# An attention and feed-forward kernel: the last token group of the first batch's q loaded apart and handled with the second batch, one PSUM tile for each x product, and the second product begun result by result

## Chip, cores and metric

The kernel runs on one core of a Trainium2 chip. The metric is the device time of one execution in microseconds (us); "span" is the time from the first to the last recorded instruction of a profiled execution, some 1.8 us shorter. A ratio compares runs of the same rounds on the same chip; the traces come from several chips, so times across rounds are compared with care.

## The reference

Shapes are 8 batches, 8 heads, 576 tokens, head size 64. All inputs and the output are float32.

```python
q_s = softmax(q over the head dimension)          # per token
k_s = softmax(k over the sequence)                # per head and channel
kv  = einsum('bhsd,bhse->bhde', k_s, v)
x   = einsum('bhsd,bhde->bhse', q_s, kv)          # -> [4608 tokens, 512]
h   = x @ w_in                                    # 512 -> 2048
g   = h + sin(alpha * h)**2 / (alpha + 1e-9)
out = g @ w_out                                   # 2048 -> 512
```

(The softmaxes subtract the maximum and divide by the sum; I have shortened them here.)

## The kernel before: the parts that matter

Each batch has 9 token groups of 64 tokens (J = 9). The feed-forward part works on tiles of 512 tokens, t = 0 to 8, so tile 0 is the first 8 groups of batch 0, and the ninth group belongs to tile 1. Every engine runs its instructions in the order of the program. The loads of batch 0, and the weights:

```python
for n, t, ii in (("q", q, 0), ("k", k, 0), ("q", q, 1), ("v", v, 0), ("k", k, 1)):
    load0(nc.sync, n, t, ii)                     # 576 KB each, all nine groups
# ... GpSimd: the rest of v, then w_in in blocks, then half of w_out
```

The x products of channels 2 and 3 share one PSUM tile of two banks, and two engines copy out of it:

```python
xp = ps_e.tile([128, 2, MF], F32, name="xp", tag="a")
for e in range(2):
    attn_chunk(0, 2 + e, 0, 8, xp[:, e])
for e in range(2):
    (DVE_CP, ACT_CP)[e](xT[:, 2 + e, 0:MF], xp[:, e])
```

First product of tile 0, for 16 outputs `ni`: matmul, sine on ScalarE, square on one of three engines (the string), combine on VectorE one output behind. Outputs 4, 5, 9, 10, 14, 15 borrow the two buffers of the pool `ps_e`; the others use the four of `ps_h`.

```python
late = {6: lambda: load("q", q, 1, ...), 8: lambda: load_wout(2),
        10: lambda: load_wout(3), 13: lambda: load("k", k, 1, ...)}
for ni in range(nN):
    h_slot(0, ni, "DPPPAPPPAPPPAPPP"[ni], lag, lent)   # D VectorE, P GpSimd, A ScalarE
    flush(lag, 1)
    if ni in late:
        late[ni]()
```

Second product of tile 0, into four accumulators, with the work for batch 1 woven in:

```python
take(os, 10);  # transposes of q's ninth group, ScalarE copies them out
take(os, 10);  # its x products, VectorE copies them out
take(os, 26)
exp_q(1); load("v", v, 1, halves=True); load_batch(2); norm_q(1, [GP, V]); exp_k(1)
# transposes of batch 1's q; cast of v by ScalarE and VectorE; table load for the sine
take(os, 8);  kv_mm(1, 0, ps_e, split=True);  kv_norm(1, 0, 1)
take(os, 2);  kv_mm(1, 1, ps_e, split=True);  kv_norm(1, 1, 2)
# ... x products of batch 1, rest of the second product, then tile 1
```

I call `kv_mm(1, 0)` and `kv_mm(1, 1)` the first and second k-v product.

The softmax here doesn't subtract the row's maximum and nothing guards it: scores larger than these inputs give would overflow.

## Time and profile before

| | before |
|---|---|
| time, median of the first 3 runs | 289.62 us (289.36 to 290.15) |
| span of the profiled run | 287.8 us |
| TensorE busy | 95% |
| TensorE begins tile 1 | 48.66 us |
| v of batch 1 lands, two halves | 42.61, 44.04 us |

The prediction below shows the page and the views that this rests on. One more stretch: TensorE around the step from the first to the second product. In a timeline, the columns are start in us, length in us, engine, line, operation, output<-inputs, shape and count; in brackets stand the idle time before and what ended it.

```profile
25.80 2.75 PE L239 MATMUL hp<-xT,win 128*128 128x512 bf16 x11
28.39 1.96 PE L239 MATMUL hh<-xT,win 128*128 128x512 bf16 x8
30.18 0.38 PE L259 MATMUL hp<-wout,g 128*128 128x512 bf16 x1
31.12 2.10 PE L259 MATMUL hp<-wout,g 128*128 128x512 bf16 x9 [0.56 <-DVE g L255]
```

Outputs 14 and 15 (`hh`) run without a wait from 28.39. After one matmul of the second product, TensorE idles 0.56 us for a combine, which frees the second accumulator.

### The profile page before, as it was taken

Reading aid. Unit: us, or ns where it says so; the run is one execution under the profiler, and the core shown is the slowest. Engines: PE = TensorE matmul, PEld = TensorE weight load, DVE = VectorE, ACT = ScalarE, POOL = GpSimd, SP = SyncE. Lnnn points to the kernel's source line nnn. Section 1 sums busy time; section 2 is a strip of 40 time slices with the busy share of each in tenths; the row PEclk is TensorE's granted clock in tenths of the full one; section 3 lists DMA queues with packets and bytes.
Section 4 is the critical chain, followed back from the end, with each engine's and each line's share of the span. In section 5 each row is a group of like instructions: output and inputs, shape, how many; then the busy total and the mean of one; then the engine's idle time right before and its main releaser. Section 6 shows DMA issues by size and latency. Waiting matters only on the chain.

```text
span 287.8 us, 4228 instructions
## 1 busy us (share of the span) xinstructions
PE 273.8 (95%) x1541; PEld 130.3 (45%) x1569; DVE 188.5 (66%) x281; ACT 225.6 (78%) x317; POOL 82.6 (29%) x78
## 2 busy tenths in 40 slices
PE   2889999999999999999999999999999999999995
PEld 1334454445454445444544454445444444444443
DVE  3948596789958567856776676747674555555412
ACT  4969656999579999899889988998877777777500
POOL 2769620676685662005300440022000000000000
PEclk9999999999999999999999999999999999999999
DMA  7999999855899958119900990115111111111142
GB/s 264 293 194 233 269 391 408 288 203 144 196 171 408 386 174 140 39 37 362 286 20 24 331 343 8 36 40 128 27 39 36 36 36 39 36 36 38 39 110 73
DMA packets 36997, 45.77 MB, mean 159 GB/s; under 512 B 15968, under 2 KB 20336, under 8 KB 36976
## 3 DMA queue, kind: packets, MB, share of 16 engines
q1 hardware_dynamic: 32304, 40.57, 46.0%
q0 software_dynamic: 4480, 4.79, 9.7%
q8 instruction: 12, 0.20, 0.3%
q10 hardware_dynamic: 192, 0.14, 0.2%
q14 instruction: 9, 0.07, 0.1%
HBM read 36.71 MB, written 9.44 MB: 160 GB/s over the span
## 4 chain that ended last, share of the span: by engine, by line
PE 87%; DVE 4%; POOL 3%; ACT 2%; issue 1%; DMA 1%
PE op L259 37%; PE hp L239 36%; PE hp L259 5%; PE kvp L162 3%; POOL s L249 2%; PE xp L211 2%; PE hh L239 2%; DMA st_q<-in_q_dram 1%; PE op L560 1%; PE op L239 1%; ACT s L245 1%; DVE qn L151 1%; DVE qs L149 1%; PE xp L219 1%; DVE g L255 1%
## 5 line engine op out<-in xcount | busy, mean ns | idle before, releaser
L255 DVE SCALAR_TENSOR_TENSOR g<-s,inva_sb,hp 128x512 bf16<-128x512 f32 x130 | 96.2, 746 | 64.6 <-ACT s L247 54.2
L239 PE MATMUL hp<-xT,win 128*128 128x512 bf16 x512 | 129.5, 379 | 1.8 <-DVE kbd L175 1.1
L259 PE MATMUL op<-wout,g 128*128 128x512 bf16 x479 | 121.8, 379 | 1.1 <-issue 0.5
L245 ACT ACTIVATE s<-hp,alpha_sb 128x512 f32<-128x512 f32 x130 | 87.7, 683 | 26.4 <-PE hp L239 24.7
L239 PEld LDWEIGHTS <-win 128*128 128x128 bf16 x576 | 56.0, 98 | 69.5 <-issue 2.1
L259 PEld LDWEIGHTS <-g 128*128 128x128 bf16 x560 | 54.1, 98 | 61.8 <-issue 1.3
L247 ACT ACTIVATE s<-s 128x512 f32<-128x512 f32 x110 | 69.3, 630 | 3.5
L151 POOL TENSOR_TENSOR qn<-qe,qs 128x1152 bf16<-128x1152 bf16 x12 | 25.3, 2128 | 74.5 <-DVE qs L145 63.4
L249 POOL TENSOR_TENSOR s<-s 128x512 f32<-128x512 f32 x31 | 32.4, 1059 | 21.9 <-ACT s L245 21.5
L265 DVE COPY o<-op 128x512 f32<-128x512 f32 (+2 forms) x33 | 22.1, 669 | 9.4 <-PE op L259 5.5
L117 ACT ACTIVATE ke<-st_k 128x1152 bf16<-128x1152 f32 x16 | 17.9, 1151 | 3.0 <-DMA st_k<-in_k_dram 3.0
L117 ACT ACTIVATE qe<-st_q 128x1152 bf16<-128x1152 f32 x16 | 17.8, 1155 | 2.4 <-DMA st_q<-in_q_dram 2.3
L144 DVE TENSOR_REDUCE qs<-qe 128x36 f32<-128x2304 bf16 x5 | 12.8, 2553 | 8.7 <-ACT qe L117 8.6
L136 POOL CAST vb<-st_v 128x1152 bf16<-128x1152 f32 x12 | 13.6, 1162 | 9.5 <-DMA st_v<-in_v_dram 9.5
L259 PE MATMUL hp<-wout,g 128*128 128x512 bf16 x62 | 15.0, 379 | 0.8 <-DVE g L255 0.6
L214 DVE CAST xT<-xp 128x512 bf16<-128x512 f32 (+1 forms) x18 | 13.4, 743 | 0.0
L162 PEld LDWEIGHTS <-ke 64*128 64x128 bf16 x288 | 8.3, 93 | 4.5 <-issue 1.5
L162 PE MATMUL kvp<-vb,ke 64*128 64x130 bf16 x288 | 9.9, 216 | 0.2 <-ACT vb L307 0.2
L117 ACT ACT_TABLE_LOAD x7 | 9.0, 1283 | 1.3 <-PEq L574 1.2
L239 PE MATMUL hh<-xT,win 128*128 128x512 bf16 x39 | 9.5, 378 | 0.2
L149 DVE TENSOR_REDUCE qs<-qe 128x18 f32<-128x1152 bf16 x6 | 8.0, 1332 | 2.2 <-ACT qe L117 2.2
L211 PE MATMUL xp<-qT,kbd 128*128 128x256 bf16 (+1 forms) x40 | 8.2, 286 | 0.4 <-DVE xT L214 0.3
(70 smaller groups left out, 117.0 us busy)
## 6 DMA issues: line engine op xcount, KB each, us to landing
out_dram<-o SPq DMA_DIRECT2D x70, 128.0 KB, 2.4
st_q<-in_q_dram SPq DMA_DIRECT2D x6, 1152.0 KB, 6.0
st_k<-in_k_dram SPq DMA_DIRECT2D x6, 1152.0 KB, 7.9
st_v<-in_v_dram SPq DMA_DIRECT2D x6, 1152.0 KB, 10.1
st_q<-in_q_dram SPq DMA_DIRECT2D x4, 576.0 KB, 6.3
st_k<-in_k_dram SPq DMA_DIRECT2D x4, 576.0 KB, 7.3
wout<-in_moe_w_out_dram POOLq DMA_DIRECT2D x4, 512.0 KB, 11.7
st_v<-in_v_dram SPq DMA_DIRECT2D x3, 576.0 KB, 9.8
```

The source lines that it names most:

```text
L117: nc.scalar.activation(dst[:, :, ii * 128:(ii + 1) * 128].rearrange("p j (x d) -> p x j d", x=2), src[:, ii::2], AX.Exp)
L136: engs[ii](vv[:, 2 * ii:2 * ii + 2, :, 0:D], staged["v", b][:, ii::2])
L151: engs[ii % len(engs)].tensor_tensor(qn[:, ii].rearrange("p j (x d) -> p j x d", x=2), qe[:, ii], part.unsqueeze(3).to_broadcast([128, J, ...
L162: nc.tensor.matmul(kvp[:, e, ii * 130:(ii + 1) * 130], ke[r, j, ii * 128:(ii + 1) * 128], vt[r, j, ii * 130:(ii + 1) * 130], start=(j == 0 ...
L211: nc.tensor.matmul(xp[:, e, 0:n], kt[:, e, ii], qT[:, ii, j0:j1, e * 64:(e + 1) * 64], start=True, stop=True)
L239: nc.tensor.matmul(hp, win[:, ki, ni * 128:(ni + 1) * 128], xT[:, ki, t * MF:(t + 1) * MF], start=(ki == 0), stop=(ki == 3))
L245: nc.scalar.activation(s, hp, AX.Sin, scale=alpha_sb[:, ni:ni + 1])
L247: nc.scalar.activation(s, s, AX.Square)
L249: nc.gpsimd.tensor_tensor(s, s, s, op=ALU.mult)
L255: nc.vector.scalar_tensor_tensor(G[t][:, ni], in0=s, scalar=inva_sb[:, ni:ni + 1], in1=hp, op0=ALU.mult, op1=ALU.add)
L259: nc.tensor.matmul(acc, G[t][:, ni, j * 128:(j + 1) * 128], wout[:, ni, :], start=(ni == 0), stop=(ni == nN - 1))
L265: eng(o[:, cols], acc)
```

## The change

The intent is to shorten the start (less of q to load and normalise before the first product), to let two engines empty the x products independently, to take load off GpSimd, and to start the second product with one free accumulator in place of two.

```diff
     for n, t, ii in (("q", q, 0), ("k", k, 0), ("q", q, 1), ("v", v, 0), ("k", k, 1)):
-        load0(nc.sync, n, t, ii)
+        load0(nc.sync, n, t, ii, 0, 8 if n == "q" else J)
 # (exponentials and normalisation of q: groups 0 to 7 alone)
-    xp = ps_e.tile([128, 2, MF], F32, name="xp", tag="a")
+    xp = [ps_e.tile([128, 2, MF], F32, name="xp", tag="a")[:, 0] for _ in range(2)]
     for e in range(2):
-        attn_chunk(0, 2 + e, 0, 8, xp[:, e])
-    for e in range(2):
-        (DVE_CP, ACT_CP)[e](xT[:, 2 + e, 0:MF], xp[:, e])
+        attn_chunk(0, 2 + e, 0, 8, xp[e])
+        (DVE_CP, ACT_CP)[e](xT[:, 2 + e, 0:MF], xp[e])
 # the second product, first quarter
-        orders = [[(n, m) for p in (0, 2) for n in R for m in (p, p + 1)], ...
+        orders = [by_m, by_n, by_n, by_m]
-        late = {6: ...
+        late = {4: load_q8, 6: ...               # two loads of 64 KB, no wait
-            h_slot(0, ni, "DPPPAPPPAPPPAPPP"[ni], lag, lent)
+            h_slot(0, ni, "DPPAPPAPPPAPPAPP"[ni], lag, lent)
-        take(os, 10); tp = ...; (transposes of group 8); ACT_CP(...)
-        take(os, 10); xp = ...; (x products of group 8); DVE_CP(...)
-        take(os, 26)
+        take(os, 46)
+        exp_to(A["qe", 0][:, 8:9], staged["q", 0][:, :, 8:9])
         exp_q(1); load("v", v, 1, ...); load_batch(2)
+        norm_q8()
         norm_q(1, [GP, V]); exp_k(1)
         (transposes of batch 1's q)
+        tp = ...; (transposes of group 8); DVE_CP(A["qT", 0][:, :, 8], tp)
         cast_v(1, [ACT_CP, DVE_CP])
         nc.scalar.activation(zero, zero, AX.Sin)
-        take(os, 8)
+        take(os, 6); xp = ...; (x products of group 8); DVE_CP(...)
+        take(os, 2)
         kv_mm(1, 0, ps_e, split=True)
```

More of the change, by code (lines that the diff above doesn't have):

```diff
@@ L122, in exp_q, with exp_half @@
         exp_to(A["qe", b], staged["q", b])
-    def exp_half(name, b, ii):
+    def exp_half(name, b, ii, j1=J):
         if ii == 0:
             A[name + "e", b] = att2.tile([128, J, 4 * D], BF16, name=name + "e")
-        exp_to(A[name + "e", b], staged[name, b], (ii,))
+        exp_to(A[name + "e", b][:, 0:j1], staged[name, b][:, :, 0:j1], (ii,))
     def exp_k(b):
@@ L136, in cast_v, with norm_q @@
             engs[ii](vv[:, 2 * ii:2 * ii + 2, :, 0:D], staged["v", b][:, ii::2])
-    def norm_q(b, engs):
-        qe = A["qe", b].rearrange("p j (ii x d) -> p ii j x d", ii=2, x=2)
+    def norm_q(b, engs, j1=J):
+        qe = A["qe", b][:, 0:j1].rearrange("p j (ii x d) -> p ii j x d", ii=2, x=2)
         A["qn", b] = qn = att1.tile([128, 2, J, 2 * D], BF16, name="qn")
@@ L146, in norm_q @@
         for ii in range(2):
-            part = qs[:, :, 2 * ii:2 * ii + 2]
+            part = qs[:, 0:j1, 2 * ii:2 * ii + 2]
             if len(engs) == 2:
@@ L150, in norm_q, with norm_q8 @@
                 nc.vector.reciprocal(part, part)
-            engs[ii % len(engs)].tensor_tensor(qn[:, ii].rearrange("p j (x d) -> p j x d", x=2), qe[:, ii],
-                                               part.unsqueeze(3).to_broadcast([128, J, 2, D]), op=ALU.mult)
+            engs[ii % len(engs)].tensor_tensor(qn[:, ii, 0:j1].rearrange("p j (x d) -> p j x d", x=2), qe[:, ii],
+                                               part.unsqueeze(3).to_broadcast([128, j1, 2, D]), op=ALU.mult)
+    def norm_q8():
+        qe = A["qe", 0][:, 8].rearrange("p (i d) -> p i d", i=4)
+        qs = small.tile([128, J, 4], F32, name="qs")[:, 0]
+        nc.vector.tensor_reduce(qs, qe, axis=AXL.X, op=ALU.add)
+        nc.vector.reciprocal(qs, qs)
+        nc.vector.tensor_tensor(qe, qe, qs.unsqueeze(2).to_broadcast([128, 4, D]), op=ALU.mult)
     def kv_mm(b, ii, pool, split=False):
@@ L322, in warm_up @@
             nc.tensor.matmul(warm, identb, A["qe", 0][:, 0:4, 0:128], start=True, stop=True)
-    exp_half("q", 0, 0)
+    exp_half("q", 0, 0, 8)
     exp_half("k", 0, 0)
-    exp_half("q", 0, 1)
+    exp_half("q", 0, 1, 8)
     warm_up(7)
-    norm_q(0, [V, V])
+    norm_q(0, [V, V], 8)
     q_tile(0)
@@ L375, in o_quad @@
         R = range(4)
-        orders = [[(n, m) for p in (0, 2) for n in R for m in (p, p + 1)],
-                  [(n, m) for n in R for m in R], [(n, m) for n in R for m in R],
-                  [(n, m) for m in R for n in R]]
+        by_m, by_n = [(n, m) for m in R for n in R], [(n, m) for n in R for m in R]
+        orders = [by_m, by_n, by_n, by_m]
         for c in R:
@@ L396, in lent, with load_q8 @@
             return ps_e.tile([128, 2, MF], F32, name="hh", tag="a")[:, 0]
-        late = {6: lambda: load("q", q, 1, halves=True, gate=DVE_CP), 8: lambda: load_wout(2),
+        def load_q8():
+            for ii in range(2):
+                load0(nc.sync, "q", q, ii, 8, 9)
+        late = {4: load_q8, 6: lambda: load("q", q, 1, halves=True, gate=DVE_CP), 8: lambda: load_wout(2),
                 10: lambda: load_wout(3), 13: lambda: load("k", k, 1, halves=True, gate=DVE_CP)}
         for ni in range(nN):
-            h_slot(0, ni, "DPPPAPPPAPPPAPPP"[ni], lag, lent)
+            h_slot(0, ni, "DPPAPPAPPPAPPAPP"[ni], lag, lent)
             flush(lag, 1)
@@ L408 @@
         os = o_quad(0, accs, [DVE_CP, ACT_CP, DVE_CP, ACT_CP])
-        take(os, 10)
+        take(os, 46)
+        exp_to(A["qe", 0][:, 8:9], staged["q", 0][:, :, 8:9])
+        exp_q(1)
+        load("v", v, 1, halves=True)
+        load_batch(2)
+        norm_q8()
+        norm_q(1, [GP, V])
+        exp_k(1)
+        for ii in range(2):
+            q_transpose(1, ii, ps_e, DVE_CP)
         tp = ps_e.tile([128, 2, 128], BF16, name="tp", tag="a")
         for ii in range(2):
-            q_transpose_ii(0, ii, 8, 9, tp[:, ii:ii + 1])
-        ACT_CP(A["qT", 0][:, :, 8], tp)
-        take(os, 10)
+            nc.tensor.transpose(tp[:, ii], A["qe", 0][:, 8, ii * 128:(ii + 1) * 128], identb)
+        DVE_CP(A["qT", 0][:, :, 8], tp)
+        cast_v(1, [ACT_CP, DVE_CP])
+        nc.scalar.activation(zero, zero, AX.Sin)
+        take(os, 6)
         xp = ps_e.tile([128, 4, P], F32, name="xp", tag="a")
@@ L418 @@
         DVE_CP(xT[:, :, 8 * P:9 * P], xp)
-        take(os, 26)
-        exp_q(1)
-        load("v", v, 1, halves=True)
-        load_batch(2)
-        norm_q(1, [GP, V])
-        exp_k(1)
-        for ii in range(2):
-            q_transpose(1, ii, ps_e, DVE_CP)
-        cast_v(1, [ACT_CP, DVE_CP])
-        nc.scalar.activation(zero, zero, AX.Sin)
-        take(os, 8)
+        take(os, 2)
         kv_mm(1, 0, ps_e, split=True)
```

## The prediction

> **What bounds the kernel now.** I read the page first, then the chain of waits in order of time for the first 50 us, then the timelines of TensorE, VectorE and the SyncE queue for the two stretches that the change touches, then the DMA share by stretch and the issues with their time to landing. On the page:
>
> ```profile
> span 287.8 us, 4228 instructions
> PE 273.8 (95%) x1541; PEld 130.3 (45%) x1569; DVE 188.5 (66%) x281; ACT 225.6 (78%) x317; POOL 82.6 (29%) x78
> DMA  7999999855899958119900990115111111111142
> ```
>
> TensorE sets the time, and its slices are full from the fourth on. The work that TensorE does is the same after the change, so only its idle time in the first 50 us can be won or lost; past that the chain is nearly all matmuls. The DMA row says the second thing: the engines are full from 3 us to about 57 us. The stretch view confirms it (columns: stretch, length, busy time and count of each engine, clock, DMA share, GB/s):
>
> ```profile
> 4.00:10.00 6.00, 4.14 (x17) 1.52 (x17) 4.18 (x4) 4.57 (x5) 3.87 (x7) 1.00 1.05 415
> ...
> 16.00:27.00 11.00, 10.61 (x48) 4.50 (x47) 7.76 (x13) 8.82 (x15) 8.59 (x10) 1.00 1.24 204
> 27.00:31.00 4.00, 3.51 (x16) 1.46 (x15) 2.30 (x5) 3.02 (x5) 3.99 (x5) 1.00 1.12 322
> 31.00:35.00 4.00, 3.88 (x19) 1.76 (x19) 2.91 (x7) 2.15 (x3) 2.26 (x3) 1.00 1.21 229
> ...
> 38.00:46.00 8.00, 7.84 (x79) 4.37 (x79) 6.82 (x11) 5.54 (x6) 2.13 (x1) 1.00 1.04 407
> ```
>
> The share is never under 1. A load that comes last in this queue therefore lands when all bytes ahead of it are through, no matter how early it was issued. The last load that TensorE needs from it is the second batch's v. The timeline of VectorE shows it arriving:
>
> ```profile
> 41.91 1.42 DVE L186 COPY qT<-tp 128x1152 bf16<-128x1152 bf16 x2 [0.34 <-PE tp L191]
> 44.06 0.76 DVE L136 CAST vb<-st_v 128x1152 bf16<-128x1152 f32 x1 [0.72 <-DMA st_v<-in_v_dram]
> 44.74 0.68 DVE L265 COPY o<-hp 128x512 f32<-128x512 f32 x1
> 45.34 0.17 DVE L172 RECIPROCAL kvr<-kvp 128x4 f32<-128x4 f32 x1
> 45.55 0.59 DVE L175 TENSOR_TENSOR kbd<-kvp,kvr 64x128 bf16<-64x128 f32 x2
> ```
>
> VectorE stands idle for 0.72 us until the second half of v lands at 44.04 (the first half landed at 42.61, is cast by ScalarE by 43.80). The chain there shows that TensorE gets to the k-v products at just that time:
>
> ```profile
> 42.38 1.73 PE hp L259 x8
> 44.11 0.62 PE kvp L162 x18
> 44.72 0.16 issue
> 44.88 0.38 PE hp L259
> 45.26 0.62 PE kvp L162 x18
> 45.88 0.32 PE hp L259
> 46.20 0.55 PE xp L219 x2
> ```
>
> The eight matmuls before end at 44.11 and the data has been ready since about 43.9: TensorE's stream and the DMA's stream are matched to 0.2 us. That is the main finding for this change: what it wins before 44 us can be spent only up to that margin.
>
> **What the skill says.** "DMA: Bandwidth & Descriptors", section "Issuing engines are not separate DMA queues": transfers from all issuers share the same 16 engines. The trace agrees: with SyncE's and GpSimd's loads together the share stays at 1.0 to 1.2. The same page, section "Specifications", gives 512 B as the smallest transfer for line rate. The trace's packet records: 2304 B in 93 ns, 2048 B in 84 ns, alpha's 512 B in 26 ns; none of 256 B, which is what the new load of q's last group is made of. "ScalarE: Activation LUTs", section "What ACT_TABLE_LOAD costs", has about 1283 ns; the page of this kernel shows 7 loads of mean 1283 ns.
>
> **The change part by part.**
> 1. Start. q's two first loads have 2048 B packets in place of 2304 B: 256 packets x 9 ns over 16 engines is 0.14 us earlier for each, 0.29 us for both. The q chain of VectorE (reductions 1.35, reciprocals 0.27, products 1.36 us, twice) becomes 8/9 as long in its two large terms: 2 x 0.30 = 0.60 us, and the first exponential drops 0.14. So VectorE is about 1 us ahead at 11.8 us. But v's second half (landed 12.72) and w_in's first block (landed 14.79, TensorE's first product began at 14.92) come by DMA. So does the next block: landed 19.45, and TensorE began on it at 19.59 after idling. The two loads of q's last group are issued with no wait behind the first five and so run at about 10 us, ahead of or among these. Estimate: 512 packets of 256 B at about 17 ns (between 9 ns for a 4 B packet and 26 ns for 512 B) over 16 engines, 0.54 us, less the 0.29 us saved: +0.25 us for every later landing; if they slip in beside larger packets at no cost, -0.29. Either way TensorE's place at 19.6 us hardly moves, by -0.2 to +0.3.
> 2. A tile for each x product. The wait of ScalarE for VectorE's copy out of the same tile (2.2 us in the waits) goes: its copy can end 0.65 us earlier, 17.05 in place of 17.72. TensorE then goes on at about 17.3 (w_in's second block landed at 16.93) and not at 17.78. It then only waits longer at 19.45 for the block after. Worth 0 to 0.13 us at that place.
> 3. Squares: 11 on GpSimd and 5 elsewhere in place of 12 and 4. GpSimd's run, which sets the combines up to 33 us, drops one 1.04 us square; ScalarE takes one 0.63 us square and has room.
> 4. Second product result by result. The combine that frees the second accumulator ended at 31.08 and TensorE idled 0.56 us for it after one matmul. With four matmuls on the first result before the second is touched, and GpSimd ahead by 0.8 us, this idle goes; TensorE, full from 19.7 at 48 x 0.216 us, begins the second product at 30.1 and does not stop. Gain at this point 0.8 to 0.9 us.
> 5. The last group's transposes, copies and products move behind 46 matmuls, with the second batch's. ScalarE's table load no longer waits for TensorE's transposes (1.7 us), so the second batch's q is ready early. TensorE would arrive at the k-v product at about 43.2 instead of 44.1.
> 6. What is there now: v still lands at 42.6 and 44.0, give or take 0.3, as it is last in the same full queue. TensorE waits 0.7 to 0.8 us and starts at about 43.9. Gain left: 0.15 us.
> 7. What is added after it: on VectorE the copy of the last group's x (0.42 us as before) now stands behind the cast of v and the output copy, and ahead of the reciprocal. And it reads the PSUM buffer that the second k-v product takes (two buffers in turn); the order of the changed kernel shows a VectorE wait at that matmul that was not there. So: landing 44.04, cast to 44.82, output copy to 45.42, x copy to about 45.80; only then the second k-v product (before: 45.19), +0.6 us. Behind it the 0.16 us hole and the 0.1 us at the x product close, so that the last part of the second product ends at 48.98 in place of 48.66: +0.3 us.
>
> Sum: +0.3 us, plus the shift of the landing, which I put at +0.1 (between -0.3 and +0.4): 289.6 + 0.4 = 290.0 us. I state 289.9, as the removed waits give a little room on the good side.
>
> **The rivals.** (a) The DMA does not hold: v lands 0.5 us or more earlier because k and v of the second batch are issued 0.4 us sooner. For it: the gate for k is a VectorE copy behind a combine that comes earlier. Against: the queue is full and the slowest engine has to do all of it. It would make 289.0 to 289.3. (b) w_out becomes the bound: its fourth block landed at 40.49 and is first needed at about 41.7 (before: 42.9), its third at 35.41 against 37.0. If SyncE's loads get a larger share earlier, it could land over 1 us later and hold TensorE ahead of the k-v product: 290.5 to 291. (c) The gain of 0.9 us stays whole, if the k-v products were held by TensorE alone: 288.7. The 0.72 us idle of VectorE for the DMA speaks against it. (d) Small packets cost 50 ns and not 17: another 1 us of DMA time, 290.8.
>
> **Range and chances.** Before's own runs spread by 0.8 us. With (a) and (c) below and (b) and (d) above I take 288.9 to 290.8. A change of 2% is 5.8 us; nothing here is of that size. Faster 0.01, same 0.98, slower 0.01.
>
> **What would show it right or wrong.** Right: in the chain, the second product starts near 30 us without the 0.56 us hole; TensorE idles 0.5 to 1 us before the first k-v product, released by the cast of v; the second k-v product waits for VectorE's copy of x; v's halves land within 0.4 us of 42.61 and 44.04; the first product of the second group starts between 48.5 and 49.3 (before 48.66). Wrong: no idle ahead of the k-v product, a landing of v before 43.5, a wait for w_out, or a start of the second group before 48.2.

## The result, and the profile after

Before: 289.63 us, median of 6 runs (289.36 to 290.15). After: 289.62 us, median of 6 (289.57 to 290.45). The ratio of after to before is 1.0004, 95% interval 0.9989 to 1.0018. (A ratio is the mean time of one kernel's fast runs over that of the other's of the same rounds, so it is not quite the ratio of the medians.) The change is worth nothing that can be measured, as predicted. The traces show that the way there was another one. (A start of tile 1 is given here as the chain of waits has it, 48.66 and 48.41; the timeline, in which matmuls overlap, shows it 0.16 to 0.17 us earlier.) First the page of the kernel after:

```profile
span 287.8 us, 4238 instructions
PE 273.6 (95%) x1541; PEld 130.9 (45%) x1569; DVE 189.1 (66%) x285; ACT 225.8 (78%) x319; POOL 81.9 (28%) x77
DMA  7999999945899957119910990115111111111142
```

It is all but the same page; only the chain and the timelines tell the two kernels apart. TensorE's timeline of the kernel after:

```profile
25.28 2.75 PE L247 MATMUL hp<-xT,win 128*128 128x512 bf16 x11
28.76 1.89 PE L247 MATMUL hh<-xT,win 128*128 128x512 bf16 x8 [0.73 <-DVE g L263]
30.48 10.09 PE L267 MATMUL hp<-wout,g 128*128 128x512 bf16 x45
40.41 1.17 PE L199 MATMUL tp<-identb,qn 128*128 128x128 bf16 x18
41.93 0.27 PE L431 MATMUL tp<-identb,qe 128*128 128x128 bf16 x2 [0.35 <-DVE qT L194]
42.04 1.46 PE L267 MATMUL hp<-wout,g 128*128 128x512 bf16 x6
...
43.98 0.68 PE L170 MATMUL kvp<-vb,ke 64*128 64x130 bf16 x18
```

The hole of 0.56 us in the second product is gone: 46 matmuls run from 30.48 without a stop. But TensorE, which was 0.5 us ahead at 25.28, waits 0.73 us at output 14 for a combine, and so starts the second product 0.3 us later than before. A second new wait of 0.35 us stands ahead of the moved transposes: they are the third tile in a pool of two buffers, and VectorE has to empty the first. The first k-v product starts at 43.98; before, it was 44.04. It does not wait for v.

Why output 14 waits is read from the timelines of GpSimd, before:

```profile
19.54 6.14 POOL L249 TENSOR_TENSOR s<-s 128x512 f32<-128x512 f32 x6 [1.59 <-ACT s L245]
25.63 0.80 POOL L110 DMA_DIRECT2D wout<-in_moe_w_out_dram  x1
26.45 2.04 POOL L249 TENSOR_TENSOR s<-s 128x512 f32<-128x512 f32 x2
```

and after, and of VectorE after:

```profile
19.16 2.04 POOL L257 TENSOR_TENSOR s<-s 128x512 f32<-128x512 f32 x2 [1.85 <-ACT s L253]
21.55 2.04 POOL L257 TENSOR_TENSOR s<-s 128x512 f32<-128x512 f32 x2 [0.35 <-ACT s L253]
24.08 2.04 POOL L257 TENSOR_TENSOR s<-s 128x512 f32<-128x512 f32 x2 [0.49 <-ACT s L253]
26.05 0.80 POOL L110 DMA_DIRECT2D wout<-in_moe_w_out_dram  x1
26.88 1.05 POOL L257 TENSOR_TENSOR s<-s 128x512 f32<-128x512 f32 x1
```

```profile
27.96 1.40 DVE L263 SCALAR_TENSOR_TENSOR g<-s,inva_sb,hh 128x512 bf16<-128x512 f32 x2 [1.07 <-POOL s L257]
```

Output 14 takes the PSUM buffer of output 9. That is free when output 9's combine is done, which needs its square. In both kernels GpSimd does six squares, then issues a w_out load for 0.80 us, and only then squares output 9. What the new pattern changes is the time before the issue: ScalarE now squares outputs 3 and 6 (at 20.26 and 22.79) ahead of the sines of outputs 4 and 7 (at 20.80 and 23.33), and GpSimd waits 0.35 and 0.49 us for these. Before, it did its six squares without a stop. So GpSimd begins 0.38 us earlier, and is 0.4 us later at the issue. Before, TensorE came to output 14 at 28.39, when the combine of output 9 (27.53 to 28.28) was just through. Now TensorE comes at 28.03, and that combine starts 0.4 us later, at 27.96.

The thirteen traces separate the two causes. From TensorE's first matmul of output 4 to the start of output 9's combine it takes 7.94 to 8.14 us in the five with the old pattern, 8.97 to 9.06 us in the three with the new one, and 8.24 to 8.25 us in the five with the new one and the load issue moved behind that square (below). The pattern costs 0.8 to 1.1 us there, and moving the issue takes 0.7 to 0.8 us of it back.

VectorE near the k-v products, after:

```profile
43.08 0.76 DVE L136 CAST vb<-st_v 128x1152 bf16<-128x1152 f32 x1 [0.35 <-DMA st_v<-in_v_dram]
43.76 0.68 DVE L273 COPY o<-hp 128x512 f32<-128x512 f32 x1
44.36 0.41 DVE L439 CAST xT<-xp 128x256 bf16<-128x256 f32 x1
44.70 0.18 DVE L180 RECIPROCAL kvr<-kvp 128x4 f32<-128x4 f32 x1
```

The second half of v landed at 43.06, almost 1 us earlier than before, so the copy of x that I expected to hold the second k-v product was done at 44.77, ahead of TensorE (45.13). Tile 1 starts at 48.41 and not at 48.66. To see how long these 0.25 us last I paired the 144 combines of the two traces in order: after is 0.26 us ahead from 55 to 67 us, and 0.05 to 0.06 us ahead from 87 us to the end. The rest is lost where TensorE needs the third batch's q, whose transposes are made by DMA. The chain there, before:

```profile
75.97 0.02 issue
75.99 0.32 PE hp L219
```

and after:

```profile
72.00 3.89 DMA qT<-qn
75.90 0.04 issue
75.94 0.32 PE hp L227
```

Before, TensorE and the transposes arrive within 0.02 us of each other. After, TensorE comes earlier, the transposes do not (landing at 75.95 before, 75.90 after), and TensorE waits.

### The profile page after: what moved, and what is told of

It reads as the page before. It is cut to its first block, busy times and chain, and to the rows that moved or that the text cites. A ratio compares the mean times of both kernels' runs of the same rounds, so it can differ in the third digit from the quotient of the medians.

```text
span 287.8 us, 4238 instructions
## 1 busy us (share of the span) xinstructions
PE 273.6 (95%) x1541; PEld 130.9 (45%) x1569; DVE 189.1 (66%) x285; ACT 225.8 (78%) x319; POOL 81.9 (28%) x77
## 4 chain that ended last, share of the span: by engine, by line
PE 85%; DMA 5%; DVE 3%; POOL 3%; issue 2%; ACT 1%; SPq 0%
PE hp L247 36%; PE op L267 34%; PE hp L267 5%; PE hh L247 2%; PE kvp L170 2%; DMA win<-in_moe_w_in_dram 2%; DMA st_k<-in_k_dram 2%; PE xp L219 2%; POOL s L257 1%; DMA qT<-qn 1%; ACT s L253 1%; PE op L571 1%; PE op L247 1%; DVE qs L149 1%; PE xp L227 1%
## 5 line engine op out<-in xcount | busy, mean ns | idle before, releaser
L257 POOL TENSOR_TENSOR s<-s 128x512 f32<-128x512 f32 x30 | 31.5, 1060 | 24.9 <-ACT s L253 24.4
L117 ACT ACTIVATE qe<-st_q 128x1152 bf16<-128x1152 f32 (+2 forms) x18 | 18.0, 1048 | 2.6 <-DMA st_q<-in_q_dram 2.6
L117 ACT ACT_TABLE_LOAD x7 | 9.0, 1283 | 1.3 <-PEq L585 1.2
L149 DVE TENSOR_REDUCE qs<-qe 128x18 f32<-128x1152 bf16 (+1 forms) x6 | 7.7, 1286 | 2.4 <-ACT qe L117 2.4
```

The source lines that it names most:

```text
L117: nc.scalar.activation(dst[:, :, ii * 128:(ii + 1) * 128].rearrange("p j (x d) -> p x j d", x=2), src[:, ii::2], AX.Exp)
L257: nc.gpsimd.tensor_tensor(s, s, s, op=ALU.mult)
```

## The experiments

I had two theories of where a gain goes. Mine from the prediction: v of batch 1 holds the k-v product at 44 us, so nothing earlier counts. The rival, from the traces: the gain is lost ahead of that, at output 14, and whatever survives is lost again at 75 us. Besides, v had landed 1 us earlier, which needed a cause. Eleven further runs were made, all correct. This is when loads landed in all thirteen traces (us; "fourth" is the fourth block of w_out):

| kernel | small q loads at start | time of the profiled run | w_out, second | w_out, fourth | v, second half |
|---|---|---|---|---|---|
| before | no | 289.59 | 30.97 | 40.49 | 44.04 |
| b_again (before) | no | 290.87 | 32.40 | 42.29 | 45.00 |
| b_rest | no | 290.67 | 31.85 | 41.80 | 44.41 |
| b_q8gate | no (at 23 us) | 290.17 | 29.43 | 40.71 | 43.89 |
| after | yes | 289.57 | 29.63 | 38.92 | 43.06 |
| a_again (after) | yes | 289.50 | 29.50 | 38.84 | 42.97 |
| b_q8 | yes | 289.65 | 28.50 | 38.03 | 42.54 |
| b_dummy | yes, besides all of q | 289.81 | 29.75 | 39.84 | 43.80 |
| a_wout10 | yes | 292.19 | 31.75 | 42.03 | 44.81 |
| a_all | yes | 294.60 | 29.80 | 39.00 | 43.16 |
| a_w10act | yes | 289.40 | 30.89 | 40.78 | 43.90 |
| a_v3early | yes | 288.68 | 29.29 | 38.46 | 42.67 |
| a_best2 | yes | 288.26 | 29.64 | 39.42 | 43.10 |

### b_again and a_again: both kernels once more

No edit. What was expected:

> The kernel before, unchanged, for a second trace. In the two traces so far the loads land earlier in the changed kernel: w_in's block for outputs 4 to 7 at 18.76 against 19.45 us, v's halves at 41.62 and 43.06 against 42.61 and 44.04. Theory A: this belongs to the change (smaller first loads, small packets). Then this run shows 19.3 to 19.6 and 42.4 to 42.8 again. Theory B: it varies from run to run by up to 1 us whatever the kernel. Then this run lies anywhere between 18.7 and 19.5, and 41.5 and 42.7.

> The changed kernel, unchanged, for a second trace. Theory A (the earlier landings belong to the change): w_in's block for outputs 4 to 7 lands at 18.6 to 18.9, v's halves within 0.2 us of 41.62 and 43.06. Theory B (run to run): elsewhere between 18.7 and 19.5. In both, TensorE waits 0.5 to 0.9 us near 28 to 29 us for the combine that frees the buffer of output 14, unless w_in comes late enough to hide it (19.45 would leave 0.1 us of it).

Measured: 290.87 us for before, 289.50 us for after, one run each (their state is unknown, as there is no second run to compare with). The kernel before landed v at 43.56 and 45.00, outside the ranges that I gave (up to 42.8 for the first half in theory A, up to 42.7 in theory B), though its w_in block landed at 19.42, inside both. TensorE waited 0.33 us for the cast of v at the first k-v product, and the span was 289.1 us in place of 287.8. The kernel after repeated itself, as theory A said: the w_in block at 18.69, v at 41.55 and 42.97, and the wait at output 14 again 0.73 us. So one kernel's v can land 1 us apart in two runs: paired with before, the combines of b_again are 0.96 us behind from 50 to 70 us, and 1.28 us from 87 us on.

### b_q8 and b_rest: the change in two halves

b_q8 is the kernel before with q's last group moved and nothing else of the change; b_rest is the kernel before with the x tiles, the squares and the order, and q as it was.

```diff
 # b_q8 = after, but:
-    h_slot(0, ni, "DPPAPPAPPPAPPAPP"[ni], lag, lent)
+    h_slot(0, ni, "DPPPAPPPAPPPAPPP"[ni], lag, lent)
-    (a tile for each x product)      -    orders = [by_m, by_n, by_n, by_m]
+    (one tile for both)              +    (pairs first, as before)
 # b_rest = before, with these three lines the other way round
```

> The kernel before with only the last token group of q moved (its own small loads, and its transposes, products and copies with the second batch); squares, x tiles and order of the second product as before. Theory A: the landings are those of the changed kernel (18.76, 41.62, 43.06). My step 4: TensorE still idles about 0.5 us for the second accumulator at 30 to 31 us. Time within 0.3 us of before: 289.4 to 289.9.

> The kernel before with the x tiles, the squares and the order of the second product, but q's last group as before. Theory A: landings as before (19.45, 42.61, 44.04), so TensorE, 0.3 to 0.6 us earlier at the k-v product, waits there for the cast of v and gains nothing: 289.5 to 289.7. Rival: the gain is lost already at 28 to 29 us, in the wait of output 14 for the combine of output 9, which stands behind GpSimd's issue of a w_out load: then that wait shows 0.3 to 0.8 us and the k-v product starts at 44.0 without a wait.

Measured: b_q8 289.72 us (median of 4), ratio to before 1.0005 (0.9970 to 1.0040); b_rest 290.34 us, ratio 1.0012 (0.9978 to 1.0046). Neither half has a measurable effect; b_rest was above the range expected for theory A (289.5 to 289.7). b_q8's loads landed still earlier than those of after (w_in block 18.05, v 41.14 and 42.54). TensorE's timeline of b_rest shows both waits in one kernel:

```profile
28.67 1.89 PE L239 MATMUL hh<-xT,win 128*128 128x512 bf16 x8 [0.73 <-DVE g L255]
...
44.26 0.69 PE L162 MATMUL kvp<-vb,ke 64*128 64x130 bf16 x18 [0.48 <-ACT vb L136]
```

It loses 0.73 us at output 14 and, as v's first half landed at 43.01 there, 0.48 us more for the cast of v. So each theory is half true of it (the rival had expected no wait at the k-v product): the wait that I had predicted does exist, where v is late. In b_q8, where v was early (41.14), TensorE started the k-v product at 44.23 with no wait, having idled 0.52 us for the second accumulator and 0.35 us for the moved transposes. b_q8 keeps the hole at the second accumulator, but it lacks the new squares as well as the new order, so it does not tell which of the two closes it. The trace of after says that the squares alone would have been enough there: the combine that frees the second accumulator (output 11's, which no longer stands behind a square of output 10 on GpSimd) ends at 30.50, 0.57 us earlier than before, and in the old order the second matmul would have been due at about 30.70 (an estimate: 30.48 and one matmul of 0.22 us). In a_wout10, below, that combine ends at 30.80 and the second product starts at 30.02; there the order is needed.

### b_dummy and b_q8gate: do the small loads bring v forward?

```diff
 # b_dummy = before, and behind the first five loads:
+    for ii in range(2):
+        spare = singles.tile([128, 2, D], F32, name=f"spare{ii}")
+        nc.sync.dma_start(out=spare, in_=(group 8 of q, batch 0)[:, ii::2])
 # b_q8gate = b_q8, and ahead of the two small loads:
+    for ii in range(2):
+        DVE_CP(staged["q", 0][:, ii, 8, 0:1], zero)     # holds them back
```

> The kernel before, all as it was, plus the two small loads (256 B packets, 64 KB each) behind the first five, into a spare tile that nobody reads. So far v's second half landed at 43.06, 42.97 and 42.54 in the three traces with q's last group moved, and at 44.04, 45.00 and 44.41 in the three without. Theory P: the small packets at about 10 us, between SyncE's and GpSimd's loads, are what brings it forward: v's second half lands at 42.5 to 43.2 here too. Theory L: it is the smaller first loads: it lands at 43.9 to 45.3 (0.5 us more of transfer). Time 289.3 to 290.3; only the landing tells.

> The kernel before with q's last group moved, but its small loads held back by a VectorE write until about 22 us, amid GpSimd's weight loads. Theory P (small packets at 10 us bring the landings forward): v's second half lands at 43.9 to 45 again. Theory L (smaller first loads do): it lands at 42.4 to 43.1. Time 289.5 to 290.5.

Measured: b_dummy's v landed at 43.80, outside both ranges; its time was 289.68 us, ratio 0.9989 (0.9976 to 1.0002). b_q8gate's v landed at 43.89, against 43.9 expected at the low end by theory P; 290.48 us, ratio 1.0022 (1.0003 to 1.0041). This is inconclusive. At this point the traces looked split (43.9 to 45.0 without the small loads at the start, 42.5 to 43.8 with them), but other runs broke the pattern: a_wout10 has them and landed v at 44.81. And a_w10act and a_v3early, which differ in nothing ahead of 65 us, landed v at 43.90 and 42.67. The landing varies from run to run by over 1 us for the same work. Whether the small loads shift its mean (44.3 over four traces without, 43.3 over nine with them, as a plain average of the table's last column, over several chips) stays open. The table shows where most of the scatter is: the three runs in which the second block of w_out landed last (31.75 to 32.40) are those with the latest v (44.41 to 45.00), and over all thirteen the two columns have a correlation of 0.92. So v's delay is largely there by 32 us, when v is only being issued; what makes it is not shown.

### a_wout10: the w_out load out of the way of output 9's square

```diff
-        late = {4: load_q8, 6: ..., 8: lambda: load_wout(2), 10: lambda: load_wout(3), ...
+        late = {4: load_q8, 6: ..., 10: lambda: (load_wout(2), load_wout(3)), ...
```

> The changed kernel with the third w_out load issued behind the square of output 9 and not ahead of it. Theory (the gain is lost first in the wait of output 14 for the combine of output 9): the 0.73 us wait of TensorE at 28 us goes, the second product starts at 29.7 to 29.8 in place of 30.4, TensorE reaches the k-v product at about 43.2. My step 7 then shows where it does not now: the second k-v product waits 0.3 to 0.5 us for VectorE's copy of x, which stands behind the cast of v (landing 43.0). The second group's first product starts at 48.0 (48.41 in the changed kernel), and some of it is lost again at 75 us, where TensorE waits for the transposes by DMA: 289.2 to 289.5. Rival (nothing before 44 us matters, v holds it): unchanged 48.4 and 289.6.

Measured: median 289.14 us of 6 runs, but from 288.91 to 292.19; ratio 0.9997 (0.9964 to 1.0030). The profile fell in the slowest of them. The wait at output 14 is gone (the group runs from 28.30 with no idle time), and the rest is as the prediction's step 7 described it, because v was late in this run (44.81):

```profile
44.56 0.69 PE L170 MATMUL kvp<-vb,ke 64*128 64x130 bf16 x18 [0.89 <-ACT vb L136]
45.40 0.38 PE L267 MATMUL hp<-wout,g 128*128 128x512 bf16 x1 [0.16 <-issue]
46.58 0.69 PE L170 MATMUL kvp<-vb,ke 64*128 64x130 bf16 x18 [0.80 <-DVE xT L439]
```

The first k-v product waits 0.89 us for the cast of v, the second 0.80 us for VectorE's copy of x behind the other cast. These are the two waits that I had forecast for the change itself. The first does not show in the change because v came early: it was cast by 42.81, before even a TensorE without the loss at output 14 would have come (43.25). The second does not show because TensorE, after that loss, came at 45.13, and the copy was through at 44.77. This run lost a further 1.1 us near 177 us, waiting for another batch's transposes by DMA; that is not in the other traces. The four runs from 288.91 to 289.24 may show what the edit gives when the loads are in time, but none of them was profiled. As a time, the edit alone is not shown to gain anything; what is shown is that the wait goes.

### a_all: three edits, one of them bad

a_wout10, and the copy of x for the last group on ScalarE ahead of its table load, and the load of the fourth batch's v behind the third batch's transposes:

```diff
-        cast_v(1, [ACT_CP, DVE_CP])
-        nc.scalar.activation(zero, zero, AX.Sin)
         take(os, 6); xp = ...; (x products of group 8)
-        DVE_CP(xT[:, :, 8 * P:9 * P], xp)
+        cast_v(1, [ACT_CP, DVE_CP])
+        ACT_CP(xT[:, :, 8 * P:9 * P], xp)
+        nc.scalar.activation(zero, zero, AX.Sin)
...
-    load("v", v, 3)
     q_transpose_dma(2, halves=True)
+    load("v", v, 3)
```

> As the run before it, and besides: the copy of the last group's x on ScalarE, ahead of its table load, so that nothing of VectorE stands between the cast of v and the second k-v product; and the load of the fourth batch's v issued behind the third batch's transposes by DMA, not ahead. Theory: no wait at the second k-v product, the second group's first product at 47.7 to 47.9, the transposes land near 73 us in place of 75.9 and TensorE does not wait for them: the whole 0.7 to 0.8 us stays, 288.8 to 289.0. Rival (another load takes the place of the ones moved, such as v of batch four for its cast): 289.4 to 289.7.

Measured: 293.39 us, ratio 1.0124 (1.0102 to 1.0145), so my expectation failed and the rival that I had named came true, only larger. Up to 65 us it went as planned: paired combines are 0.93 us ahead of before, and tile 1 starts at 47.73. The transposes landed at 72.78 and 74.19. But the fourth batch's v landed at 78.97, and GpSimd, in order, did nothing else meanwhile:

```profile
79.09 2.27 POOL L136 CAST vb<-st_v 128x1152 bf16<-128x1152 f32 x2 [9.29 <-DMA st_v<-in_v_dram]
81.32 4.21 POOL L151 TENSOR_TENSOR qn<-qe,qs 128x1152 bf16<-128x1152 bf16 x2
85.49 3.04 POOL L257 TENSOR_TENSOR s<-s 128x512 f32<-128x512 f32 x3
```

Its squares for tile 2 began at 85.49 (80.95 before), the combines waited for them, and the kernel ended 5.0 us behind.

### a_w10act: without the bad edit

a_all with the load of v where it was.

> The changed kernel with two edits: the third w_out load issued behind the square of output 9, and the copy of the last group's x on ScalarE ahead of its table load. v's load for the fourth batch stays where it was. Theory: up to 65 us TensorE is 0.7 to 0.9 us ahead of the kernel before, as in the run that had the 5 us loss; at 75 us it waits for the third batch's transposes by DMA, which land at 75.2 to 75.9 whatever TensorE does, and keeps 0.1 to 0.4 us: 289.2 to 289.5 in fast runs. Rival (the transposes come forward with the work that issues them): the whole 0.7 to 0.9 us stays, 288.7 to 288.9.

Measured: median 289.08 us of 6 (288.73 to 290.55), ratio to before 0.9974 (0.9949 to 0.9998), between the two ranges that were expected. It differs from a_all by the load of v alone, so that load is what cost a_all its time (about 4 us between the two medians, which are of different rounds). In the profiled run v was late (42.41 and 43.90), TensorE waited 0.60 us for its cast at the first k-v product, and there was none at the second. The paired combines are 0.58 us ahead from 55 to 64 us and 0.22 us ahead from 87 us on: the transposes landed at 75.73, and TensorE waited for them, as it was expected to.

### a_v3early: the fourth batch's v earlier, not later

```diff
     exp_q(2)
+    load("v", v, 3)
     exp_k(2)
...
-    load("v", v, 3)
     q_transpose_dma(2, halves=True)
```

> As the run before it, and the fourth batch's v is loaded about 1 us earlier: issued behind the third batch's q exponentials, ahead of two output stores, so that it waits for the cast of the third batch's v alone. Theory (the transposes by DMA stand in the queue behind this 1152 KB load): v of batch four lands near 73 in place of 73.8, the transposes near 75.0 in place of 75.9, and 0.3 to 0.7 us more of the gain stays than in the run before it: 288.7 to 289.0. Rival (the transposes are set by their own issue): the same time as the run before it.

Measured: median 288.76 us of 6 (288.50 to 289.32), ratio 0.9957 (0.9935 to 0.9979). The load was issued at 65.94 (68.12 before) and landed at 71.98 (73.88), the transposes at 73.87 and 75.02 (75.01 and 75.95). The paired combines are 1.08 us ahead up to 64 us and 0.93 us ahead from 87 us on. So most of what is won early now survives the point at 75 us, as expected from the theory that the transposes stand behind that load in the queue. The rival (their own issue sets them) is not quite excluded by this run: against a_w10act the second transpose was issued 0.27 us earlier and landed 0.71 us earlier. a_all is the clearer evidence: with the load behind them, the second transpose took 2.87 us from issue to landing, against 3.69 us in before. v of the second batch was early in this run, so part of the 1.08 us is luck.

### a_best2: the moved transposes four matmuls later

```diff
         (transposes of batch 1's q)
+        take(os, 4)
         tp = ...; (transposes of group 8); DVE_CP(A["qT", 0][:, :, 8], tp)
-        take(os, 6); xp = ...
+        take(os, 2); xp = ...
```

> As the run before it, and the two transposes of q's last group come four matmuls later, so that TensorE does not wait 0.35 us for VectorE to empty the PSUM buffer that they take. Theory: that 0.35 us wait goes and TensorE gets to the k-v product at 43.0; where v's first half lands at 41.6 this stays, 0.2 to 0.35 us better than the run before it; where it lands at 43 (as in about half of the traces) the k-v product waits for the cast of v and nothing is won. Median 288.5 to 289.0, with single runs up to 291.

Measured: median 288.55 us of 6 (287.83 to 289.99), ratio 0.9952 (0.9926 to 0.9978). The wait ahead of the transposes is gone, and now v is what TensorE meets:

```profile
41.23 0.28 PE L432 MATMUL tp<-identb,qe 128*128 128x128 bf16 x2
...
42.84 0.69 PE L170 MATMUL kvp<-vb,ke 64*128 64x130 bf16 x18 [0.24 <-ACT vb L136]
```

v's first half landed at 41.60 and was cast by 42.80. The paired combines are 1.39 us ahead from 55 us and 1.37 us from 87 us on. The arrival was better than expected (42.60 and not 43.0), so that even an early v makes TensorE wait. This is the best version that I ran: about 0.5% under before, with an interval that excludes no change, and lower than the change's 289.62 us, though the two did not run in the same rounds. Against a_v3early it is not proved better (288.55 to 288.76 us, overlapping runs).

## Why the prediction was right or wrong

The time (289.9 predicted, 289.62 measured) and the class were right, and the measured median is well inside the range. The steps were not all. Two of the four signs of being wrong came: no idle time ahead of the k-v product, and a landing of v before 43.5.

- **Where the bound is.** Right: TensorE's stream sets the end, everything that the change can win lies ahead of 50 us, and another stream takes it back. Step 6 named the wrong place for this run.
- **Step 1, the start.** Half right. VectorE was to be about 1 us ahead at 11.8; its last product of q ended at 11.53 and not at 11.77, only 0.24 us ahead. The instructions were shorter as computed (1.35 and 1.36 us became 1.22 and 1.23), but q's loads did not land earlier (4.70 and 7.66, before 4.53 and 7.50). The estimate of 17 ns for a packet of 256 B was good (18 ns measured). The bound that "TensorE's place at 19.6 us hardly moves, by -0.2 to +0.3" failed: it began the block at 18.91 and not at 19.59, as the w_in block landed at 18.76 and not at 19.45. The landing varies more than the effect that I computed: 18.76 occurs in b_rest too, which has q's loads as before.
- **Step 2, the x tiles.** ScalarE's copy ended at 17.10 (17.05 predicted). I gave it 0 to 0.13 us because the next block would come late. As that came early, it is worth more: b_q8, without the separate tiles, began that block at 19.23 though it had landed at 18.05, and b_rest with them began at 18.90 on a landing of 18.76.
- **Step 3, the squares.** This is the step that failed. I counted squares (one fewer on GpSimd) and took it that GpSimd would be 0.8 us ahead. The square that is dropped (output 10's) stands behind output 9's; up to that one GpSimd has as much to do as before, and now waits 0.84 us for two sines that stand behind ScalarE's squares. So output 9's combine starts 0.4 us later, TensorE comes to output 14 0.36 us earlier, and waits 0.73 us for that buffer. a_wout10 removed the wait by moving the load issue alone, which lies ahead of output 9's square in both kernels.
- **Step 4, the order.** Right in that the 0.56 us hole is gone in after and b_rest and stays in b_q8. That the order closed it is not shown: order and squares never ran apart, and in after the squares would have been enough. The gain at that point was predicted as 0.8 to 0.9 us with the second product at 30.1; it began at 30.48, because of step 3.
- **Step 5.** The table load and the second batch's q came early as predicted. The arrival at the k-v product was predicted for 43.2 and was 43.98. Of the 0.78 us, the wait of step 3 and the 0.35 us for the third tile in a pool of two buffers are more than enough; I had not looked at the pool. In a_v3early, without the first of these, it was 43.15.
- **Step 6, v.** Wrong for the change: v landed at 41.62 and 43.06 (my margin was 0.3 us, I had written that a landing before 43.5 would prove me wrong), and the k-v product did not wait. Right as a mechanism: b_rest, a_wout10, a_w10act and a_best2 wait there, by 0.48, 0.89, 0.60 and 0.24 us. The mis-sized term is the spread of the landing, which I took from one trace.
- **Step 7, the copy of x.** The wait was predicted for the change and appears only in a_wout10 (0.80 us), where v came at 44.81, and in b_q8gate (0.32 us), where it came at 43.89. The order of instructions was read correctly; its start time was not. In after, tile 1 begins at 48.41, below my 48.5 to 49.3.
- **What I had not foreseen.** A second place, at 75 us, where DMA meets TensorE: it took 0.2 of the 0.26 us that were left. It was visible in the chain before as an idle time of 0.02 us, that is, as a tie.
- **The rivals.** (a) came nearest: v was earlier by 1 us. Its reason is not shown, as v was issued only 0.16 to 0.21 us sooner and its landing scatters by more. Its time of 289.0 to 289.3 us did not come, because of step 3 and the point at 75 us. (b) and (d) did not show. (c) is what the later kernels partly reach.

So the number came out right by luck, by two errors of opposite sign: v came 1 us better than I assumed, and the squares cost 0.73 us that I had not seen.

## What to carry to other kernels

When one stream is sped up in a tuned kernel, look in the chain for every later point where another stream arrives within a few tenths of a microsecond of it; each such tie takes back part of what was won, and a gain lasts only as far as the next tie. Here each tie that was moved in turn let more of it through (0.22, 0.93 and 1.37 us at the end in the traces of a_w10act, a_v3early and a_best2, part of it the luck of an early v). Before changing which engine does a piece of work, write down that engine's whole order, load issues included, and follow what each item waits for and what it frees; a count of the pieces is not enough. And take the landing time of a load in a full queue from several traces: here one trace was off by as much as the whole effect.

## What the Trainium skill lacked or had wrong

- "DMA: Bandwidth & Descriptors", section "Specifications", gives 512 B as the smallest transfer for line rate. The packet records of the kernel after (medians; 2048 B for q's first loads): 256 B in 18 ns, 512 B in 25 ns, 2048 B in 84 ns, 2304 B in 93 ns; so 14, 20, 24 and 25 B/ns. The trace agrees that 256 B is slow, but its 512 B packets (alpha's 16, the only ones) did not reach the rate of the large ones either.
- The same page, section "Issuing engines are not separate DMA queues", is confirmed (the share stays at 1.0 to 1.2 with two issuers). I found nothing on how far a landing scatters when both issue at once: v's second half landed between 42.54 and 45.00 us over thirteen traces, at 44.04 and 45.00 for one unchanged kernel. What sets it stays open here.
- The same section says that the issue time saved is usually small relative to the transfer. That holds relative to the transfer (a w_out load took 8.5 to 13.1 us from issue to landing in after), but for an engine that also computes it is not the measure: a w_out issue took 0.74 to 0.80 us of GpSimd, about three quarters of a square (1.04 us), and moving one removed a 0.73 us wait of TensorE.
- "ScalarE: Activation LUTs", section "What ACT_TABLE_LOAD costs", is right on the load itself: 1283 ns mean here.
